# Dense products in column tiles behind a value block, in a two-layer attention and GLU kernel

## The chip, the cores and the metric

The kernel runs on one core of a Trainium2 chip. The metric is the device time of one execution in microseconds; a version's time is the median of three runs. A profile is taken of one further execution, and its trace gives the start of every instruction.

## What is computed

Two equal layers of sliding-window attention and a gated feed-forward part over 2,048 tokens of width 512, in bfloat16, with a layer norm without weights ahead of each part:

```python
def _A_ref(x, wqkv, wo):
    H = 32; Dh = D // H; W = 256          # D = 512, Dh = 16, S = 2048
    q, k, v = ...                          # x @ wqkv, by heads
    scores = jnp.einsum("bhqd,bhkd->bhqk", q, k) * (Dh ** -0.5)
    mask = (idx[:, None] - idx[None, :] >= 0) & (idx[:, None] - idx[None, :] < W)
    p = _softmax(jnp.where(mask[None, None], scores, -1e9), axis=-1)
    o = jnp.einsum("bhqk,bhkd->bhqd", p, v)
    return heads_joined(o) @ wo

def _B_ref(x, w_gate, w_up, w_down):       # F = 1792
    h = _sigmoid(x @ w_gate) * (x @ w_up)
    return h @ w_down

x = x + _A_ref(_layernorm(x), A_wqkv, A_wo)
x = x + _B_ref(_layernorm(x), B_w_gate, B_w_up, B_w_down)
x = x + _A_ref(_layernorm(x), A_wqkv, A_wo)
x = x + _B_ref(_layernorm(x), B_w_gate, B_w_up, B_w_down)
```

Both layers use the same weights. All weights and the residual `xsb` stay in SBUF for the whole run.

## The kernel before

**Tiles.** Tokens go in 16 tiles of 128 per layer. A query tile sees its own key tile and the two before it. PE (TensorE) works in three tilings:

- *dense products* use the whole 128 x 128 array: q and k (`q_unit` L768, `k_unit` L799), v (`v_unit` L838), gate and up (`glu_units` L863, product at L871), down (`down_units` L924, product at L935) and the output projection (`oproj_unit` L962, product at L966). One step is one matmul of 128, 256 or 512 columns; a unit's steps accumulate in one of four PSUM banks.
- *scores* (`scores` L1075) use four row tiles of 32 x 128, one for each of four heads' key slices, and write the tile `Sps`, four PSUM banks that all visits share. A *visit* is one such block for a key tile and a quarter of the heads (kind "A") or for the window's edges (kind "R"); there are 154 in the two layers. After each comes one exponential on ACT (L1155) over 128 x 2048 elements, which empties `Sps` into the ring `PTring` or into `edge`.
- *values* (`values` L1157, product at L1182) use four column tiles of 128 x 32: one block is 16 heads of one query tile, 80 matmuls (fewer for a layer's first two tiles) of 64 or 128 columns in groups of four, each with a `tile_position` of (0, 32g) and its own weights of 32 columns. There are 64 blocks.

Results leave the banks by copies on ACT or DVE, tanh on ACT and a fused multiply on DVE (L889, L897) for gate and up, and adds on DVE. Transposes of normed rows and of the attention's output go by DMA on SP's queue, but for the first tiles, which go by PE.

**Order.** No engine's order is written out by hand. While the program is built, a planner (`Plan`, L211) keeps a time for each engine with a table of costs, and each engine takes the ready task of the lowest priority number (`dispatch` L249). PE asks `pick` (L1279): a score visit if its inputs are there, the exponential before has ended and a pace has passed; else a value block whose probabilities are masked (`do_values` L1346), as a rule straight after a score visit; else one step of a dense unit from `choose` (L1414). The planner counts instructions, since PE's code comes in blocks of 256 (`count`, `held`, `issue`, L350 to L371), and it charges a fixed cost where the mode goes from one of "d", "s" and "pv" to another (`matmul` L391). The priorities, slacks, ranks and the pace are numbers in `SEGMENTS` (L94), with one set for the start of each stretch of visits; `OPT`, `RANK`, `EARLY` and `GLU` hold further choices. In the program that results, all that is fixed; at run time engines wait only for each other's semaphores.

The planner's numbers are what it plans with; they are not measurements.

The step of a dense unit, before:

```python
ns, fn = u.steps[u.at]
pl.count(1)
end = pl.matmul("d", ns)
fn()
```

Of the kernel before, what the change touches and what calls it, by code (L numbers as in the profile page):

```python
# [56 lines left out]
def pool_ns(n):  # L57
# [2 lines left out]

EXP_NS = 1880
TAIL = (384, 128)
GLU = [[[1, 1, 1, 1, 2, 2], [1, 1, 1, 1, 2, 2], [1, 1, 1, 1, 2, 2], [1, 1, 1, 1, 1, 1, 1, 1], [2, 2, 2, 2], [1, 1, 2, 2, 2], [2, 2, 4]], [[4, 4, 4, 2, 1, 1], [4, 4, 4, 1, 1, 2], [4, 4, 4, 4]]]
EARLY = 12
FILL = 800
OVERLAP = {"ACT": 114, "DVE": 83, "POOL": 45, "SP": 0}
LATENCY = {"ACT": 45, "DVE": 40, "POOL": 60, "SP": 0}
# [11 lines left out]
FETCH = (1200, 2300)  # L79


OPT = dict(gu='SP', g1=1, bk=3, bq=2, wide=0, r0=2, g0=2, g2=2, x0=1, eps=1, hold=0, own=1, ck=0, cq=2, turn=2,
    split=0, mo=0, r1=0, near=0)
RANK = dict(x3=33548.83335140428, wd=1211.7000995894928)


class Late(dict):


    def __missing__(self, name):  # L90
# [1 line left out]


SEGMENTS = {  # L94
    0: (False, dict(st_x0=13.863, ap_x0=3.152, xt_x0=9.296, st_x1=3.154, ap_x1=7.542, xt_x1=6.357, st_x=14.008,
        ap_x=13.772, xt_x=-3.395, st_p=0.711, ap_p=14.553, xt_p=4.622, st_g=-2.573, ap_g=-1.639, xt_g=-3.705,
        st_g0=2.021, ap_g0=-16.439, xt_g0=-6.334, tp=9.915, tp_g=2.607, q=-4.446, q0=12.608, q1=-11.166, k=-12.623,
        k0=2.155, k1=0.919, s=-5.392, s0=-1.662, s1=-1.49, v=5.412, v0=19.01, v1=20.238, vv=6.697, exp=-6.258,
        exp0=-3.822, m0=0.08, m00=3.447, e0=-5.468, e00=2.019, e1=3.572, e10=7.186, m2=1.966, m20=4.281, th=10.065,
        mu=-9.464, dn=-12.991, add=-5.529, add0=6.323, out=-9.784, mv=27.065, mv0=4.046, oq=-1.002, oq0=-4.981,  # L100
        no=2.541, no0=-9.565, on=10.323, on0=-6.623, vc=8.609, vc0=1.087), dict(xt=2480, oq=333, on=656, vc=2033),
        dict(tp=-12.366, o=-7.523, lead=12.467, far=66.411, v=2.907, g=58.132, d=22.245, feed=32.11,
        x3=33548.83335140428, wd=1211.7000995894928, go=147.06927590305332), 622.2),
    5: (False, {}, {}, {}, 622.2),
    10: (False, {}, {}, {}, 622.2),
    12: (False, {}, {}, {}, 2218.12),
    15: (False, {}, {}, {}, 2218.12),
    20: (False, {}, {}, {}, 2218.12),
    25: (True, dict(st_p=1.759, ap_p=37.537, xt_p=1.918, st_x=-0.666, ap_x=-8.548, xt_x=10.765, st_g=-9.429,
        ap_g=-8.046, xt_g=17.53, q=-9.886, k=11.998, s=-2.346, v=-6.167, exp=-28.375, m0=5.963, e0=7.951, e1=8.163,  # L110
        m2=6.893, th=-3.899, mu=-14.418, dn=5.971, add=-16.001, out=22.687, mv=28.405, oq=-3.007, no=5.357, on=9.644,
        vc=-13.067), dict(xt=205, oq=2779, on=3180, vc=6577), dict(tp=25.318, o=-33.126, lead=9.136, far=25.67, v=1.764,
        g=13.215, d=13.271, feed=-39.311, go=2154.735913081243), 2702.16),
    30: (False, {}, {}, {}, 2702.16),
    35: (False, {}, {}, {}, 2702.16),
    40: (False, {}, {}, {}, 2702.16),
    45: (False, {}, {}, {}, 2702.16),
    50: (False, {}, {}, {}, 2702.16),
    55: (False, {}, {}, {}, 2702.16),
    60: (False, {}, {}, {}, 2702.16),  # L120
    65: (False, {}, {}, {}, 2702.16),
    70: (False, {}, {}, {}, 2702.16),
    75: (False, {}, {}, {}, 2702.16),
    80: (False, {}, {}, {}, 2591.1),
    85: (False, {}, {}, {}, 3017.42),
    90: (False, dict(oq=-4.09), {}, dict(o=-30.75, lead=9.62, v=1.47), 2875.9),
    95: (False, dict(oq=-3.007), {}, dict(o=-33.126, lead=9.136, v=1.764), 3017.42),
    100: (False, {}, {}, {}, 3017.42),
    105: (False, {}, {}, {}, 3017.42),
    110: (False, {}, {}, {}, 3017.42),  # L130
    115: (False, dict(xt_x=13.72, m0=9.31), {}, {}, 2984.3),
    120: (False, dict(xt_x=10.765, m0=5.963), {}, {}, 3017.42),
    125: (False, {}, {}, {}, 3017.42),
    130: (False, {}, {}, {}, 3017.42),
    135: (False, {}, {}, {}, 3017.42),
    140: (False, {}, {}, {}, 3017.42),
    145: (False, {}, {}, {}, 3017.42),
    150: (False, {}, {}, {}, 3017.42),
}


# [270 lines left out]
class Net:  # L412


    def __init__(self, ctx, tc, A_x, wqkv, wo, w_gate, w_up, w_down, out):
# [37 lines left out]
        self.rms = [big.tile([P, 1], F32, name=f"rm{e}") for e in range(2)]  # L453
        self.bufs = {}
        self.slot = 0

        def ring(name, n, shape, dt=BF16):
            self.bufs[name] = [[big.tile(shape, dt, name=f"{name}{i}"), True] for i in range(n)]
# [306 lines left out]
    def cut(self, L, g, cq, n):  # L765
        return ((0, NBG - 1), (NBG - 1, 1)) if L == g == 0 and cq < n else ((0, NBG),)

    def q_unit(self, L, g, cq, i0, n):  # L768
        nc, pl, key = self.nc, self.pl, ("p", L, g)
        t0, gi = g * NBG + i0, L * NTG + g  # L770

        by_tile = L == g == 0 and cq < OPT["bq"]
        w = P if by_tile else n * P

        def steps(bank):
            return [(mm_ns(w), lambda kt=kt, o=o: nc.tensor.matmul(  # L776
                self.banks[bank][:, o:o + w], lhsT=self.wq[:, kt, cq * P:cq * P + P],
                rhs=self.xnT[key][0][:, i0 + o // P:i0 + (o + w) // P, kt, :],
                start=kt == 0, stop=kt == KT - 1)) for o in range(0, n * P, w) for kt in range(KT)]

        def evac(u):
            u.done.then(lambda: self.used(key, 1))
            at = gi % QG * TGW + i0 * P
            d = pl.task({"ACT": act_ns(n * P), "DVE": dve_ns(n * P)}, lambda e: self.copy(
                e, self.qT[:, cq, at:at + n * P].rearrange("p (t z k) -> p t z k", z=2, k=HP),
                self.banks[u.bank][:, 0:n * P].rearrange("p (t k z) -> p t z k", z=2, k=HP)), [u.done], self.prio["q" + self.phase(L, g)])
            d.done.then(lambda: [self.q_ready[L, t, cq].fire() for t in range(t0, t0 + n)])
            return d.done

        tiles = [self.xn_ready[key, t] for t in range(t0, t0 + n)]  # L790
        needs = [self.has_wq["q"]] + ([] if by_tile else tiles)
        if gi >= QG:
            needs.append(self.seen[divmod((gi - QG) * NBG + NBG - 1, NT)])
        u = Unit(("q", L, g, cq if i0 == 0 else cq + 3), steps, needs, False, evac)
        if by_tile:
            u.want = [e for e in tiles for kt in range(KT)]
        return u

    def k_unit(self, L, g, cq, i0, n):  # L799
# [4 lines left out]
        w = P if by_tile else n * P  # L804

        def steps(bank):
            return [(mm_ns(w), lambda kt=kt, o=o: nc.tensor.matmul(  # L807
                self.banks[bank][:, o:o + w], lhsT=self.wq[:, kt, D + cq * P:D + cq * P + P],
                rhs=self.xnT[key][0][:, i0 + o // P:i0 + (o + w) // P, kt, :],
                start=kt == 0, stop=kt == KT - 1)) for o in range(0, n * P, w) for kt in range(KT)]  # L810
# [27 lines left out]
    def v_unit(self, L, t):  # L838
# [1 line left out]
        key, gi, o = ("p", L, g), L * NTG + g, (t % NBG) * P  # L840

        def steps(bank):
            return [(mm_ns(D), lambda kt=kt: nc.tensor.matmul(  # L843
                self.banks[bank][:], lhsT=self.xnT[key][0][:, t % NBG, kt, :], rhs=self.wq[:, kt, 2 * D:3 * D],
                start=kt == 0, stop=kt == KT - 1)) for kt in range(KT)]

# [16 lines left out]
    def glu_units(self, L, t0, n, c0):  # L863
# [4 lines left out]

        def mms(bank, wts, fcs):
            pt = self.banks[bank][:, 0:len(wts) * len(fcs) * w].rearrange("p (i f w) -> p i f w", i=len(wts), w=w)  # L870
            return [(mm_ns(w), lambda i=i, j=j, fc=fc, wt=wt, kt=kt: self.nc.tensor.matmul(  # L871
                pt[:, i, j, :], lhsT=wt[:, kt, fc * P:(fc + 1) * P], rhs=self.xnT[key][0][:, q0:q0 + n, kt, :],
                start=kt == 0, stop=kt == KT - 1))
                for i, wt in enumerate(wts) for j, fc in enumerate(fcs) for kt in range(KT)]
# [49 lines left out]
    def down_units(self, L, t, t0, n, c0):  # L924
# [4 lines left out]
        def unit(o, w):  # L929
# [2 lines left out]

            def mm(bank, fc):
                at = (c0 * GW + fc * n * P + (t - t0) * P) % (HCH * GW)
                nc.tensor.matmul(self.banks[bank][:, 0:w], lhsT=self.hT[:, at:at + P], rhs=self.wd[:, fc, d],  # L935
                                 start=fc == 0, stop=fc == FC - 1)
                if t == t0 + n - 1 and end:
                    pl.at(pl.pe_free + PE_LATENCY, self.h_used[L, t0, fc].fire)
# [23 lines left out]
    def oproj_unit(self, L, t, b):  # L962
        nc, pl = self.nc, self.pl

        def steps(bank):
            return [(mm_ns(D), lambda c=c: nc.tensor.matmul(  # L966
                self.banks[bank][:], lhsT=b[0][:, c, :], rhs=self.wot[:, c, :],
                start=c == 0, stop=c == KT - 1)) for c in range(KT)]

# [309 lines left out]
    def pick(self):  # L1279
# [20 lines left out]
                    t < 2 or self.v_hi[L, t - 2].fired):  # L1300
                pv = self.pv_list[0]
        held = s < len(self.visits) and s > 0 and self.exps[s - 1].ends is None
        if visit and pl.mode == "pv" and go <= 0:
            if go > 0:
                return False
            wait = go
        elif pv and (pl.mode != "d" and 1 or wait <= -1 or wait > 1e8 or held):
            return self.do_values(pv, spare)
# [2 lines left out]
            u = self.choose()  # L1311
        if visit and (wait <= 0 or go <= 0 and u is None):
            self.last_s = pl.now
            end = pl.matmul("s", self.scores(*visit))
            pl.at(end, self.s_done[s].fire)
            self.exps[s] = self.visit_exp(s)
# [15 lines left out]
                return True  # L1332
            return False
        ns, fn = u.steps[u.at]
        pl.count(1)
        end = pl.matmul("d", ns)
        fn()
        u.at += 1
        if u.at == 1 and u.begin:
# [3 lines left out]
            pl.at(end, u.done.fire)  # L1343
        return True

    def do_values(self, pv, spare):  # L1346
        pl = self.pl
        self.pv_list.pop(0)
        bank = min(spare, key=lambda i: self.bank_turn[i])
        self.bank_user[bank] = Unit(("v alues",), None, [], False, None)  # L1350
        end = pl.matmul("pv", self.values(*pv, bank))
# [241 lines left out]
```

## Time and profile before

| | us |
|---|---|
| median of three runs | 540.58 |
| lowest, highest | 539.96, 541.48 |
| profiled execution: whole time | 542.07 |
| profiled execution: span of the trace | 540.4 |

The mean granted clock of TensorE in the profiled execution is 0.999. The profile's page cuts the span into 40 slices of 13.5 us; a digit is the busy share in tenths:

```profile
PE   6999999999999999999999999999999999999997
PEld 5446654866757544444444445444444445444443
DVE  5899989889897888678978978878967866552332
ACT  2999979978989798787787886788858774330320
```

PE is short of full in the first slice and the last alone. ACT and DVE are nearly full in the first third and have room afterwards; past some 455 us no visit is left, and PE runs dense products to the end. Engine names on the page: PE is TensorE's matmul, PEld its weight loads, DVE VectorE, ACT ScalarE, POOL GpSimd, SP the engine that issues most DMAs. The busy time of PE holds overlapping matmuls, so what a matmul costs is read from the distance of two starts.

The costliest groups on PE, by shape:

```profile
L935 PE MATMUL bank<-wd,hT 128*128 128x512 bf16 x434 | 105.7, 380 | 0.0
L871 PE MATMUL bank<-xnT,wu 128*128 128x512 bf16 x336 | 89.0, 379 | 0.0
L871 PE MATMUL bank<-xnT,wg 128*128 128x512 bf16 x336 | 87.8, 380 | 0.0
L1182 PE MATMUL bank<-PTring,Vaug 128*32 128x64 bf16 x1920 | 47.7, 193 | 0.0
L1182 PE MATMUL bank<-PTring,Vaug 128*32 128x128 bf16 x960 | 45.0, 223 | 0.0
```

The columns are line, engine, operation, tile written and tiles read, the array tile, the output's shape, the count, busy us and mean ns of one, and idle time before. The mean of 380 ns for a product of 512 columns includes the time from entry to end of one matmul; the next one starts long before that.

### The profile page before, as it was taken

To read this page: it belongs to the slowest core of one execution; us is meant where nothing else is said; L and a number is where in the kernel's file an instruction comes from. 1 tells how busy PE (TensorE), PEld (TensorE's weight loads), DVE (VectorE), ACT (ScalarE), POOL (GpSimd) and SP (SyncE) were. 2 spreads that over 40 slices of the span, in tenths; PEclk is the share of its full clock that TensorE was granted. 3 is DMA by queue.
4 is the path that set the end of the run, shared out by engine and by line. 5 is a ranking of instruction groups with operands and counts; after the bars stand their busy time and mean duration, and the time that the engine had idled before them with its cause. 6 is when DMAs were issued, how large, how long until landed. Compare 5 with 4: busy or idle time off the path is not lost.

```text
span 540.4 us, 21116 instructions
## 1 busy us (share of the span) xinstructions
PE 529.0 (98%) x9536; PEld 279.7 (52%) x9536; DVE 411.0 (76%) x820; ACT 385.9 (71%) x377; POOL 43.6 (8%) x99
## 2 busy tenths in 40 slices
PE   6999999999999999999999999999999999999997
PEld 5446654866757544444444445444444445444443
DVE  5899989889897888678978978878967866552332
ACT  2999979978989798787787886788858774330320
POOL 3411001000001010000000101001000001000000
PEclk9999999999999999999999999999999999999999
DMA  8843533224332225223112612062222512411001
GB/s 261 310 113 74 100 73 51 54 51 92 33 61 43 61 42 111 33 60 72 42 32 52 101 41 43 18 105 59 45 51 52 83 29 52 69 19 40 1 12 39
DMA packets 95083, 36.22 MB, mean 67 GB/s; under 512 B 78352, under 2 KB 93968, under 8 KB 94992
## 3 DMA queue, kind: packets, MB, share of 16 engines
q1 hardware_dynamic: 93872, 33.82, 29.7%
q8 instruction: 74, 1.21, 0.9%
q10 hardware_dynamic: 1120, 1.05, 0.7%
q14 instruction: 17, 0.14, 0.1%
HBM read 9.70 MB, written 2.10 MB: 22 GB/s over the span
## 4 chain that ended last, share of the span: by engine, by line
PE 90%; DMA 3%; ACT 3%; DVE 2%; issue 1%; SPq 1%; POOL 0%; ACTq 0%
PE bank L871 37%; PE bank L935 18%; PE bank L1182 8%; PE Sps L1102 7%; PE bank L966 5%; PE bank L776 4%; PE bank L807 4%; PE bank L843 4%; PE Sps L1113 2%; DMA xnT<-xn 2%; ACT PTring L1155 1%; DMA wq<-in_A_wqkv_dram 1%; SPq L527 1%; DVE st L645 0%; DVE PTring L1033 0%
## 5 line engine op out<-in xcount | busy, mean ns | idle before, releaser
L1155 ACT ACTIVATE PTring<-Sps 128x2048 bf16<-128x2048 f32 (+1 forms) x122 | 226.1, 1853 | 48.5 <-PE Sps L1102 44.0
L871 PE MATMUL bank<-xnT,wu 128*128 128x512 bf16 (+2 forms) x672 | 125.0, 308 | 0.0
L871 PE MATMUL bank<-xnT,wg 128*128 128x512 bf16 (+2 forms) x672 | 123.6, 309 | 0.4 <-DMA xnT<-xn 0.4
L897 DVE SCALAR_TENSOR_TENSOR hT<-hT,bank 128x512 bf16<-128x512 bf16 (+1 forms) x140 | 78.9, 576 | 44.7 <-PE bank L871 36.4
L889 ACT ACTIVATE hT<-bank 128x512 bf16<-128x512 f32 (+1 forms) x140 | 69.8, 514 | 56.3 <-PE bank L871 55.8
L935 PE MATMUL bank<-wd,hT 128*128 128x512 bf16 (+2 forms) x462 | 108.8, 373 | 0.0
L871 PEld LDWEIGHTS <-wu 128*128 128x128 bf16 x672 | 55.9, 98 | 40.5 <-issue 2.5
L871 PEld LDWEIGHTS <-wg 128*128 128x128 bf16 x672 | 55.0, 98 | 41.8 <-issue 3.0
L1155 ACT ACTIVATE edge<-Sps 128x2048 bf16<-128x2048 f32 (+1 forms) x32 | 56.8, 1774 | 16.5 <-PE Sps L1113 16.5
L935 PEld LDWEIGHTS <-hT 128*128 128x128 bf16 x462 | 42.6, 98 | 48.2 <-issue 1.2
L1033 DVE TENSOR_TENSOR PTring<-PTring,mask 128x1024 bf16<-128x1024 bf16 x64 | 43.6, 683 | 11.7 <-ACT PTring L1155 11.6
L1182 PE MATMUL bank<-PTring,Vaug 128*32 128x64 bf16 (+1 forms) x2880 | 51.5, 203 | 0.0
L1182 PEld LDWEIGHTS <-Vaug 128*32 128x32 bf16 x2880 | 43.8, 97 | 11.6 <-issue 9.5
L1102 PE MATMUL Sps<-qT,kTp 32*128 32x256 bf16 (+3 forms) x1216 | 47.4, 248 | 0.8 <-ACT edge L1155 0.4
L736 DVE CAST OTs<-bank 128x512 bf16<-128x512 f32 x50 | 36.4, 729 | 13.8 <-PE bank L1182 13.4
L645 DVE BATCH_NORM_STATS2 st<-xsb 128x6 f32<-128x512 bf16 x64 | 43.9, 687 | 3.4 <-DMA xsb<-in_A_x_dram 2.7
L658 POOL TENSOR_SCALAR st<-st 128x2 f32<-128x2 f32 (+1 forms) x33 | 11.3, 344 | 424.6 <-DVE st L647 424.4
L1182 PE MATMUL bank<-edge,Vl 128*32 128x64 bf16 x1024 | 44.4, 193 | 0.0
L1033 DVE TENSOR_TENSOR edge<-edge,maske 128x1024 bf16<-128x1024 bf16 x60 | 39.9, 681 | 1.3 <-ACT edge L1155 1.2
L1102 PEld LDWEIGHTS <-kTp 32*128 32x128 bf16 x1216 | 17.8, 92 | 44.0 <-issue 42.1
L1182 PE MATMUL bank<-edge,Vh 128*32 128x64 bf16 x896 | 40.6, 193 | 0.0
L1033 DVE TENSOR_TENSOR PTring<-PTring,maskn 128x1024 bf16<-128x1024 bf16 x56 | 38.2, 682 | 0.7 <-ACT PTring L1155 0.7
(76 smaller groups left out, 523.7 us busy)
## 6 DMA issues: line engine op xcount, KB each, us to landing
Vl<-Vaug SPq DMA_DIRECT2D x32, 68.0 KB, 2.7
out_dram<-xsb SPq DMA_DIRECT2D x15, 128.0 KB, 2.1
Vh<-Vaug SPq DMA_DIRECT2D x28, 68.0 KB, 2.6
wg<-in_B_w_gate_dram SPq DMA_DIRECT2D x2, 896.0 KB, 8.6
wu<-in_B_w_up_dram SPq DMA_DIRECT2D x2, 896.0 KB, 12.1
wd<-in_B_w_down_dram SPq DMA_DIRECT2D x7, 256.0 KB, 4.4
xsb<-in_A_x_dram SPq DMA_DIRECT2D x6, 256.0 KB, 7.0
wq<-in_A_wqkv_dram ACTq DMA_DIRECT2D x3, 256.0 KB, 5.7
```

The costliest lines, as they stand in the source:

```text
L645: nc.vector.bn_stats(out=st[:, 0:6], in_=self.xsb[:, t, :])
L736: self.nc.vector.tensor_copy(out=out, in_=in_)
L776: return [(mm_ns(w), lambda kt=kt, o=o: nc.tensor.matmul(self.banks[bank][:, o:o + w], lhsT=self.wq[:, kt, cq * P:cq * P + P], rhs=self.xn ...
L871: return [(mm_ns(w), lambda i=i, j=j, fc=fc, wt=wt, kt=kt: self.nc.tensor.matmul(pt[:, i, j, :], lhsT=wt[:, kt, fc * P:(fc + 1) * P], rhs= ...
L889: self.nc.scalar.activation(out=self.hT[:, ch[0] * GW:ch[0] * GW + size], in_=pt, func=AF.Tanh, scale=0.5)
L897: self.nc.vector.scalar_tensor_tensor(out=h, in0=h, scalar=1.0, in1=pt, op0=ALU.add, op1=ALU.mult)
L935: nc.tensor.matmul(self.banks[bank][:, 0:w], lhsT=self.hT[:, at:at + P], rhs=self.wd[:, fc, d], start=fc == 0, stop=fc == FC - 1)
L966: return [(mm_ns(D), lambda c=c: nc.tensor.matmul(self.banks[bank][:], lhsT=b[0][:, c, :], rhs=self.wot[:, c, :], start=c == 0, stop=c == ...
L1033: done = pl.task({"DVE": dve_bf_ns(1024)}, lambda e: nc.vector.tensor_tensor(out=r, in0=r, in1=m.to_broadcast([P, 16, HP]), op=ALU.mult), ...
L1102: nc.tensor.matmul(self.sps[:, m, o:o + n * HP], lhsT=kTp[32 * m:32 * m + 32, i, tt, e, :], rhs=self.qT[32 * m:32 * m + 32, i, q0:q0 + n * ...
L1155: nc.scalar.activation(out=out, in_=src, func=AF.Exp, scale=scale)
L1182: nc.tensor.matmul(o, lhsT=Va[:, c0:c0 + 32], rhs=p(h), start=k == 0 or t == 0, stop=k == len(parts) - 1 or t == 0, tile_position=(0, 32 * g))
```

## The change

Two things change. First, a dense step that is picked while PE is in the values' tiling (mode "pv"), with the next score visit less than `ranks["col"]` (about 2.5 us of the plan) away, is issued as four matmuls of 32 weight columns each, in the same four column tiles that values use, and PE's mode stays "pv". At most 16 such steps follow each other. Transposes on PE never run so. The products and their accumulation in the bank are the same. Second, the planner's numbers are others, so that all engines' orders are planned anew.

```diff
-GLU = [[..., [1, 1, 1, 1, 2, 2], [1, 1, 1, 1, 1, 1, 1, 1], ...]]
-EARLY = 12
+GLU = [[..., [1, 1, 1, 1, 1, 1, 2], [1, 1, 1, 1, 1, 1, 1, 1], ...]]
+EARLY = 8
...
-OPT = dict(gu='SP', g1=1, bk=3, bq=2, wide=0, r0=2, g0=2, g2=2, x0=1, eps=1, hold=0, own=1, ck=0, cq=2, turn=2,
-    split=0, mo=0, r1=0, near=0)
-RANK = dict(x3=33548.83335140428, wd=1211.7000995894928)
+OPT = dict(gu='SP', g1=1, bk=3, bq=2, wide=0, r0=2, g0=0, g2=2, x0=1, eps=1, hold=1, own=1, ck=0, cq=2, turn=2,
+    split=0, mo=0, col=16, near=0, r1=1)
+RANK = dict(x3=32849.91338862893, wd=1289.5079568774777)
...
+    def mm(self, out, lhsT, rhs, start, stop):
+        if not self.col:
+            self.nc.tensor.matmul(out, lhsT=lhsT, rhs=rhs, start=start, stop=stop)
+            return
+        for g in range(4):
+            q = slice(32 * g, 32 * g + 32)
+            self.nc.tensor.matmul(out[q], lhsT=lhsT[:, q], rhs=rhs, start=start, stop=stop, tile_position=(0, 32 * g))
...
-            return [(mm_ns(D), lambda kt=kt: nc.tensor.matmul(
+            return [(mm_ns(D), lambda kt=kt: self.mm(
...
-        if visit and pl.mode == "pv" and go <= 0:
-            if go > 0:
-                return False
+        if visit and pl.mode == "pv" and go <= 0 and not self.runs:
             wait = go
...
         ns, fn = u.steps[u.at]
-        pl.count(1)
-        end = pl.matmul("d", ns)
+        near = min(wait, go if self.pv_due() else 1e9)
+        self.col = pl.mode == "pv" and u.name[0] != "tp" and near < self.ranks["col"] and self.runs < OPT["col"]
+        self.runs = self.runs + 1 if self.col else 0
+        pl.count(4 if self.col else 1)
+        end = pl.matmul("pv" if self.col else "d", ns + 3 * self.col)
         fn()
...
+    def pv_due(self):
+        return False
```

The same exchange of `nc.tensor.matmul` for `self.mm` stands in the q, k, v, gate and up, down and output products. `runs` is set to 0 at a score visit and at a value block. `SEGMENTS` has new numbers throughout (for one, the pace at the first visits goes from 622 to 2463 and later from 3017 to 2914). The entry of `GLU` that `g0` names is the same list in both, so the token groups of gate, up and down are unchanged. `hold=1` lets the norm statistics of tiles 2 and 3 wait for tiles 0 and 1. `x3` and `wd` are when the last tokens and the pieces of the down weights are asked for: the last tokens at 32.8 us of the plan instead of 33.5, the last piece at 63.8 instead of 62.6.

## The prediction

> **What bounds the kernel now.** First the page: busy times, the queue that carries PE's code, the shares of the chain of waits, and the row of the exponentials.
>
> ```profile
> PE 529.0 (98%) x9536; PEld 279.7 (52%) x9536; DVE 411.0 (76%) x820; ACT 385.9 (71%) x377; POOL 43.6 (8%) x99
> ...
> q8 instruction: 74, 1.21, 0.9%
> ...
> PE 90%; DMA 3%; ACT 3%; DVE 2%; issue 1%; SPq 1%; POOL 0%; ACTq 0%
> ...
> L1155 ACT ACTIVATE PTring<-Sps 128x2048 bf16<-128x2048 f32 (+1 forms) x122 | 226.1, 1853 | 48.5 <-PE Sps L1102 44.0
> ```
>
> PE is busy 98% of the span and holds 90% of the chain; no other engine passes 76%. So the time is PE's own sequence plus what interrupts it, and every number below is a change of one of these two. The second line counts 74 loads of code. PE runs 2 x 9,536 = 19,072 loads and matmuls, 258 per code load.
>
> Next the timeline of PE over one round, since the change is about how PE goes from one tiling to another.
>
> ```profile
> 301.71 0.81 PE L871 MATMUL bank<-xnT,wu 128*128 128x512 bf16 x3
> 302.45 0.40 PE L1102 MATMUL Sps<-qT,kTp 32*128 32x256 bf16 x8
> 302.78 0.27 PE L1182 MATMUL bank<-PTring,Vaug 128*32 128x128 bf16 x8
> 302.87 0.20 PE L1182 MATMUL bank<-edge,Vh 128*32 128x64 bf16 x4
> 302.90 0.20 PE L1182 MATMUL bank<-PTring,Vaug 128*32 128x64 bf16 x4
> 302.93 0.20 PE L1182 MATMUL bank<-edge,Vl 128*32 128x64 bf16 x4
> 302.96 0.26 PE L1182 MATMUL bank<-PTring,Vaug 128*32 128x128 bf16 x8
> ...
> 303.45 0.20 PE L1182 MATMUL bank<-edge,Vl 128*32 128x64 bf16 x4
> 303.59 1.04 PE L871 MATMUL bank<-xnT,wg 128*128 128x512 bf16 x4
> 304.46 1.03 PE L871 MATMUL bank<-xnT,wu 128*128 128x512 bf16 x4
> 305.42 0.41 PE L1113 MATMUL Sps<-qT,kTp 32*128 32x64 bf16 x32
> ```
>
> The first column is the start, and starts are what counts, since matmuls overlap. Four dense 512-column products take 304.46 - 303.59 = 0.87 us, 0.216 each (the median over 1,391 such gaps). Four value products of 64 columns, one in each tile of 32 columns, take 0.029 (302.87 to 302.90). Where the tiling changes, the gap is longer: 303.45 to 303.59 is 0.14 where 0.03 would do. Over the trace, the starts on either side of a change put it above plain streaming by 111 ns for values to dense, 98 for dense to scores, 104 for scores to dense, 100 for scores to values, 110 for values to scores (one case).
>
> Third, an interruption on the same timeline:
>
> ```profile
> 59.64 0.61 PE L871 MATMUL bank<-xnT,wg 128*128 128x128 bf16 x8
> 60.09 0.61 PE L871 MATMUL bank<-xnT,wu 128*128 128x128 bf16 x8
> 60.53 0.27 PE L871 MATMUL bank<-xnT,wg 128*128 128x128 bf16 x2
> 60.74 0.26 PE L1113 MATMUL Sps<-qT,kTp 32*128 32x64 bf16 x10
> 61.73 0.35 PE L1113 MATMUL Sps<-qT,kTp 32*128 32x64 bf16 x22 [0.73 <-issue]
> ```
>
> At 60.8 PE stops 0.9 us in the middle of a score visit, waiting for nothing that the profile shows ("issue"). A load on the code queue began at 59.36 and ended at 60.28; PE went on 1.4 us later. The closest starts of two code loads in the trace are 3.48, 3.56 and 3.65 us apart. So 258 instructions can't go faster than about 3.6 us, and values followed by short products try to. The page's last line above sets a second floor: all visits write one score tile, so a visit waits for the exponential (1.85 us) of the one before; the shortest distance of two visits' starts in the trace is 2.41 us.
>
> I also laid the order of before out by these prices: streaming plus changes of tiling come to 522.3 us. Of what the trace has beyond that, 7.8 us lie before 28 us (start, first loads). After 28 us some 1.5 us are stops on code, 1.7 us are other waits (ACT, xnT, OnT) and 1.9 us are small change.
>
> **The change, part by part.** The program's order of after against before:
>
> 1. *Changes of tiling.* Before has 372, after 323. Values to dense fall from 58 to 6 (52 x 111 = -5.77 us), dense to scores from 151 to 99 (52 x 98 = -5.10), values to scores rise from 3 to 55 (52 x 110 = +5.72), scores to dense by 3 and scores to values fall by 3 (+0.01), dense to values rise by 3 (3 x 100 = +0.30). The sum is -4.84; the 49 plain gaps that come back at 2.5 ns make it **-4.7 us**. The price of values to scores rests on one case, but it lies beside values to dense (111).
>
> 2. *Dense products in column tiles.* 504 steps (362 of 512 columns, 67 of 256, 75 of 128) become four matmuls each; columns streamed stay equal. A dense step of 128 columns takes 56 ns (60.09 - 59.64 over 8). In the values' tiling, four matmuls of 128 columns and four of 64 take 85 to 90 ns (302.96 to the next row, left out, at 303.05), 29 of them for the 64, so again 56 to 58. I take 0. A column-tiled stream wider than 128 is not in the trace. Bounds: 504 x -2.5 = -1.3 us, if the step lost its gap; +5.5 us, if it behaved like the wide score groups (four of 256 columns in row tiles take 120 ns, 11 more than a dense 256): 504 x 11. I take 0 because columns are the nearer row.
>
> The Trainium skill speaks against this step: "TensorEngine Tiling (Array Packing)", section Instruction Overhead, says each matmul carries about 60 cycles and that the tiling factor should not come from a small dimension. At 2.4 GHz four would need 100 ns, so by it the 75 short steps would lose 44 ns each, 3.3 us (an estimate from that page). The trace's 29 ns for four matmuls contradict it, and the sum does without it.
>
> 3. *Code.* 1,512 more matmuls and as many weight loads are 3,024 instructions, 11.7 more code loads. PE's price per 258 instructions falls from 7.1 to 6.1 us on average, which hides them; what counts is where they crowd. Values (160 instructions in 0.70 us) are now followed by steps of eight instructions. I cut PE's order into pieces of the code loads' size and priced each by the rows above, with visits held 2.41 us apart. Before has four pieces under 5 us, the shortest 3.56. After has nineteen: 2.07, 2.40, 2.86, 2.97, 3.26, 3.54, 3.86, 3.90, and eleven from 4.07 to 4.92. At 3.6 us per load the first six lack 1.53 + 1.20 + 0.74 + 0.63 + 0.34 + 0.06 = 4.5 us, against before's 1.5 in the trace: **+3.0 us**. Bounds: -1.5 (all hidden) and +7.6, if each load needs 4.2 us (it took 4.7 from where PE came near the boundary to the end of the stop at 60.8): then the pieces lack 9.1. A stop on code holds everything behind it on PE, the next score visit first; that visit's exponential is then late too, which ACT (71% busy) can bear.
>
> 4. *The new order.* Its start is the same to 28 us, step for step. ACT, DVE, POOL and SP keep their work: 384 instructions on ACT for 385, 823 on DVE for 822, 104 on POOL and 190 on SP in both, transfers among them; who copies what and when is dealt anew. All of it is hidden under PE (71 and 76%) unless PE waits. After 28 us, ten distances between visits are now priced under 2.41 us: 2.18, 1.75, 2.26, 2.04, 2.27, 2.27, 1.54, 2.11, 2.05, 2.16. They lack 3.5 us in all, 1.3 of it at three places where code is late as well, so 2.2 remain. I add 0.7, less than half of the old other waits, for waits inside longer distances, and take off the old 1.7: **+1.2 us**. Bounds: 0 (they merely replace the old ones) and +2.2 (they come on top). The down weights' last piece is asked for at 63.8 us instead of 62.6 and lands some 4.4 us after; its product came at 69 us and comes about 71 now. Without that cover it costs 1.2 us at most.
>
> Sum: -4.7 + 0 + 3.0 + 1.2 = **-0.5 us**. The profiled execution took 542.07 us, 540.4 of it span; the median of three runs is 540.58, so the profile reads 1.5 us high and only the difference carries over: 540.58 - 0.5 = 540.1 us. Of this kernel a measurement can tell about 0.3% (1.6 us) from no change: faster means below 538.9, slower above 542.2.
>
> **The rivals.**
>
> *The saving stands* (faster). Code comes in time, because stops fall where PE waits for an exponential anyway, and the new waits half replace the old, so a third of step 3's 3.0 us and half of step 4's 1.2 are paid: -4.7 + 1.0 + 0.6 = -3.1, **537.5 us**. For it: three of the ten short distances already coincide, and a piece priced 3.56 us in before's trace passes without a stop. Against it: pieces of 2.1 and 2.4 us can't be met at any spacing that the trace shows. Chance 0.35.
>
> *Code loading decides* (slower). One mechanism: after a value block PE runs through its code faster than it is delivered. In before a load started up to 2 us after PE came near its boundary, most often just behind value blocks, where after puts its new instructions. At 4.1 us per load the pieces lack 8.0 us: -4.7 + 6.5 + 1.2 = +3.0, **543.6 us**. It decides from about 3.93 us per load on (a lack of 6.6). For it: 60.8 us in the trace. Against it: most loads there started 1.1 us after the boundary came near. Chance 0.21.
>
> *Column tiles stream slower when wide* (slower): the score groups' 11 ns per step, -0.5 + 5.5 = +5.0, **545.6 us**. Against it: their overhead stays at 2 to 3 ns from 64 to 128 columns. Chance 0.05.
>
> That the change does nothing is out: the order shows 2,016 dense matmuls in tiles of 32.
>
> **How the numbers follow.** The forecast, within 0.3%, has 0.37; other mishaps on the slow side 0.02. So faster 0.35, same 0.37, slower 0.28. The likeliest case's own range, 538.9 to 542.2, is the band. The range for 8 in 10 reaches halfway into both rivals' own spread, from 536.3 (-4.3: saving whole, 0.4 lost) to 543.6 (the code rival's time): about 0.1 stays out on either side.
>
> **What would show it.** Right: PE's gap behind a value block is one group's, not 0.14; a four-tile step of 512 columns takes 216 ns; some 86 code loads; PE waits after 28 us of about 7 us instead of 3, half of them "issue" between 90 and 120 us. Wrong: four-tile steps above 220 ns (step 2), waits under 4 us (the faster rival), code waits over 7 us (the slower), or dense products that wait on xnT or hT, which the sum doesn't hold.

## The result, and the profile after

The changed kernel is slower. Seven runs of each on the same chip gave medians of 546.07 us (544.58 to 547.16) for after and 541.48 us (539.96 to 543.49) for before: ratio 1.008, 95% interval 1.0055 to 1.0105. That is less than 2%, but clear of the scatter of the runs. The ratios, here and below, are estimated from all the runs and can differ from the quotient of the medians (1.0085 here); each experiment was measured beside before on one chip, not always the chip of the other experiments, so kernels are compared by their ratios to before. The profiled execution of after has a span of 544.3 us, before's had 540.4.

The page of after, with the lines that answer to those shown of before (busy time of each engine, the code queue, the shares of the chain of waits, the row of the exponentials):

```profile
PE 521.6 (96%) x10993; PEld 283.4 (52%) x11048; DVE 411.6 (76%) x821; ACT 385.4 (71%) x376; POOL 43.1 (8%) x99
...
q8 instruction: 86, 1.41, 1.1%
...
PE 84%; DVE 7%; ACT 3%; issue 3%; POOL 1%; DMA 1%; ACTq 0%; DVEq 0%
...
L1167 ACT ACTIVATE PTring<-Sps 128x2048 bf16<-128x2048 f32 (+1 forms) x122 | 225.9, 1852 | 46.9 <-PE Sps L1114 42.3
```

PE's share of the chain fell from 90 to 84%, "issue" rose from 1 to 3% and DVE from 2 to 7%. Code loads rose from 74 to 86. The other engines' work is nearly unchanged. (55 of the 11,048 matmuls have no record; they were placed by their weight loads.) The timeline of PE over one round, at the place that the change is about:

```profile
297.34 0.20 PE L1194 MATMUL bank<-PTring,Vaug 128*32 128x64 bf16 x4
297.37 0.20 PE L1194 MATMUL bank<-edge,Vl 128*32 128x64 bf16 x4
297.39 0.39 PE L778 MATMUL bank<-xnT,wu 128*32 128x512 bf16 x4
297.61 1.04 PE L778 MATMUL bank<-xnT,wg 128*32 128x512 bf16 x16
298.48 0.61 PE L778 MATMUL bank<-wd,hT 128*32 128x512 bf16 x8
298.91 0.39 PE L778 MATMUL bank<-xnT,wu 128*32 128x512 bf16 x4
299.23 0.40 PE L1114 MATMUL Sps<-qT,kTp 32*128 32x256 bf16 x8
```

The step behind the value block starts 0.02 to 0.03 us after it (297.37 to 297.39), not 0.14. Sixteen matmuls of 512 columns are four steps and take 298.48 - 297.61 = 0.87 us, the same as four whole products before. The change of tiling has moved to the scores: 298.91 to 299.23 is 0.32 us, 0.216 of it streaming. So the edit does what it says, at the price foreseen. What went wrong is in the waits of PE. Before has one row of "issue" in that view, of 0.7 us, and none of its waits for exponentials is longer than 0.4:

```profile
PE Sps L1113 <- issue: 0.7, 1, 0.7
PE Sps L1102 <- ACT edge L1155: 0.4, 1, 0.4
```

After, the longest sums:

```profile
PE bank L774 <- issue: 5.3, 21, 1.4
PE bank L778 <- issue: 1.4, 2, 0.8
PE bank L1194 <- issue: 1.2, 2, 1.0
...
PE Sps L1125 <- issue: 0.8, 1, 0.8
PE bank L1194 <- DVE PTring L1045: 0.8, 1, 0.8
```

Each row is what waited, for what, us in total, times, longest. The first row has seeming waits of 0.16 us too, behind products whose record is missing. One of the "issue" rows' waits on the timeline:

```profile
107.91 0.62 PE L778 MATMUL bank<-xnT,wu 128*32 128x128 bf16 x32
108.46 0.34 PE L774 MATMUL bank<-xnT,wg 128*128 128x128 bf16 x3
108.73 0.40 PE L1114 MATMUL Sps<-qT,kTp 32*128 32x256 bf16 x8
110.54 0.44 PE L774 MATMUL bank<-xnT,wg 128*128 128x128 bf16 x5 [1.41 <-issue]
```

Behind eight short tiled steps (32 matmuls in 0.55 us), three short whole ones and a score visit PE stands for 1.4 us and waits for nothing shown. A load on the code queue ended at 109.29, 1.26 us before PE went on.

I laid PE's order out by the prediction's prices and sorted what each trace has beyond them: the time to 28 us; stops on code; waits of over 0.15 us that the profile names, after 28 us; the rest. About 4.9 us at both ends of the span are the same in all. By this sort before has 1.1 us of code stops and 1.2 us of named waits, where the prediction counted 1.5 and 1.7. The table has the kernels of the experiments too:

| us | span | priced work | to 28 us | code stops | named waits | rest |
|---|---|---|---|---|---|---|
| before | 540.4 | 522.3 | 7.8 | 1.1 | 1.2 | 3.1 |
| after | 544.3 | 517.6 | 6.8 | 8.3 | 3.8 | 2.9 |
| E1: new order, no tiles | 548.4 | 522.6 | 6.8 | 3.6 | 6.1 | 4.5 |
| E2: old order, all tiles | 552.6 | 517.4 | 8.0 | 15.8 | 3.9 | 2.8 |
| E7: new order, chosen tiles | 541.0 | 519.8 | 7.6 | 0.0 | 5.9 | 2.8 |
| E8: old order, chosen tiles | 538.9 | 519.0 | 8.3 | 0.6 | 3.4 | 2.7 |

Before to after: -4.7 of priced work, +7.2 of code stops, +2.6 of named waits, -1.0 at the start and -0.2 of rest make +3.9 us, the difference of the spans.

### The profile page after: what moved, and what is told of

It is laid out like the page before. It is cut to its first block, busy times and chain, and to the rows that moved or that the text cites. A ratio compares the mean times of both kernels' runs of the same rounds, so it can differ in the third digit from the quotient of the medians.

```text
span 544.3 us, 24074 instructions
## 1 busy us (share of the span) xinstructions
PE 521.6 (96%) x10993; PEld 283.4 (52%) x11048; DVE 411.6 (76%) x821; ACT 385.4 (71%) x376; POOL 43.1 (8%) x99
## 3 DMA queue, kind: packets, MB, share of 16 engines
q10 hardware_dynamic: 1120, 1.05, 0.6%
## 4 chain that ended last, share of the span: by engine, by line
PE 84%; DVE 7%; ACT 3%; issue 3%; POOL 1%; DMA 1%; ACTq 0%; DVEq 0%
PE bank L774 52%; PE bank L778 15%; PE bank L1194 8%; PE Sps L1114 6%; ACT PTring L1167 2%; PE Sps L1125 2%; DVE st L649 1%; DVE PTring L1045 1%; DMA xsb<-in_A_x_dram 1%; DVE kTp L834 1%; POOL st L663 1%; DVE xn L681 1%; DVE edge L1045 1%; DVE xsb L984 0%; DVE kTp L740 0%
## 5 line engine op out<-in xcount | busy, mean ns | idle before, releaser
L774 PE MATMUL bank<-xnT,wu 128*128 128x512 bf16 (+2 forms) x552 | 102.0, 307 | 0.3 <-issue 0.2
L774 PE MATMUL bank<-xnT,wg 128*128 128x512 bf16 (+2 forms) x518 | 96.2, 309 | 2.4 <-issue 2.2
L774 PE MATMUL bank<-wd,hT 128*128 128x512 bf16 (+2 forms) x349 | 81.5, 371 | 2.4 <-issue 1.3
L1167 ACT ACTIVATE edge<-Sps 128x2048 bf16<-128x2048 f32 (+1 forms) x32 | 56.7, 1771 | 13.3 <-PE Sps L1125 12.7
L774 PEld LDWEIGHTS <-wu 128*128 128x128 bf16 x552 | 45.8, 98 | 34.9 <-issue 2.8
L774 PEld LDWEIGHTS <-wg 128*128 128x128 bf16 x518 | 42.9, 98 | 36.2 <-issue 5.4
L774 PEld LDWEIGHTS <-hT 128*128 128x128 bf16 x376 | 35.3, 98 | 40.3 <-issue 2.1
L774 PE MATMUL bank<-xnT,wq 128*128 128x512 bf16 (+1 forms) x256 | 48.7, 330 | 0.6 <-DMA wq<-in_A_wqkv_dram 0.4
```

The costliest lines, as they stand in the source:

```text
L774: self.nc.tensor.matmul(out, lhsT=lhsT, rhs=rhs, start=start, stop=stop)
L1167: nc.scalar.activation(out=out, in_=src, func=AF.Exp, scale=scale)
```

## The experiments

E1 to E4 ask which part of the change costs the time, E5 to E10 test a rule for the stops that came out of the first traces.

**E1: the new order without column tiles.** After, with the branch for four tiles switched off; the order of all engines is after's.

```diff
-        if not self.col:
+        if True:
             self.nc.tensor.matmul(out, lhsT=lhsT, rhs=rhs, start=start, stop=stop)
             return
```

Expected: 

> The new order kept instruction for instruction, but every dense product issued on the whole array again: 1,512 matmuls and 1,512 weight loads fewer, 375 changes of tiling instead of 323. Theory (code arrives late): the changed kernel's stops at the code boundaries, 8.3 us in its trace, fall to 1.5 or less, the tiling costs 5.0 us more by the trace's prices (522.6 instead of 517.6 us), so 1 to 2 us less than the changed kernel: about 544 us, some 2 us over before, which is what the new order's other waits cost. Rival (the new order's own waits make the loss, not the tiles): the loss of 8.6 us in waits stays and 5.0 us come on top, about 551 us.

Measured: 550.16 us against 542.64, ratio 1.0138 (1.0118 to 1.0159). So the first theory's 544 us is out and the rival's 551 is met: the new order without the tiles that it was planned with costs more than the whole change. The rival's number is met, but only part of its account: of the 8.0 us that E1's span has over before's, 4.9 are named waits, 2.5 are code stops and most of the rest is matmuls at a lower clock. Its priced work is before's, and it has 6.1 us of named waits instead of 1.2: a mask that a value block waits for at 44 us (0.80), transposes that wait for their sources between 45 and 48 us (1.3 in sum), an exponential at 111 us (0.89), a dense step at 95.5 us (1.2). One code stop of 2.3 us is followed by a stretch of matmuls at half speed. In the view of PE's waits:

```profile
PE bank L1194 <- issue: 2.4, 2, 2.1
PE Sps L1114 <- ACT PTring L1167: 1.8, 5, 0.8
```

**E2: column tiles in the old order.** Before, with every dense step between a value block and the next visit (at most 16 of them, no transposes) in four tiles. These are 542 steps, 2,168 tiled matmuls in the trace; where the expectations of E8 and E9 say 532, it is 542.

```diff
+        self.tiles = 0 if u.name[0] == "tp" else max(self.tiles - 1, 0)
         fn()
...
         self.pv_list.pop(0)
+        self.tiles = 17
```

Expected: 

> The order of before kept, and the dense steps behind a value block (at most 16, until a score visit or a transpose) issued in four column tiles: 1,626 matmuls more than before, 321 changes of tiling instead of 372, priced 517.4 instead of 522.3 us. Theory (code arrives late): the old order was not made for the extra code, so stops at the code boundaries grow by 8 to 17 us; less 4.9 us for the tiling, 545 to 553 us. Rival (the new order's waits make the loss): the saving of 4.9 us shows, about 536.5 us.

Measured: 554.12 us, ratio 1.0219 (1.02 to 1.0237). Priced work falls by 4.9 us as in after, and code stops rise to 15.8 us at fourteen places. The rival's gain is out; the tiles without the new order are worse still, and the reason is code.

**E3: after with code moved.** Each of the 54 warm-up products, which compute nothing, is cut in two: 108 more instructions ahead of everything, the rest of PE's order untouched.

```diff
-        for i in range(n):
-            nc.tensor.matmul(self.banks[bank][:, 0:P], lhsT=self.hT[:, 0:P], rhs=self.hT[:, 0:P], start=True, stop=True)
+        for i in range(2 * n):
+            nc.tensor.matmul(self.banks[bank][:, 0:P // 2], lhsT=self.hT[:, 0:P], rhs=self.hT[:, 0:P // 2], start=True, stop=True)
```

Expected: 

> The changed kernel with each of the 54 warming products of the start (128 columns) split into two of 64: 108 instructions more ahead of everything, the same work on the array, so the code blocks' boundaries fall 0.42 of a block elsewhere in an otherwise equal order. Theory (code arrives late): the stops leave their places (99, 103, 110, 118, 178, 222, 275 us) and reappear where the shifted boundaries lie, again 0.8 of a block in; their sum stays between 5 and 11 us, the time within 4 us of the changed kernel. Rival (the stops belong to the work at those places): same places, same lengths, same time within 0.3%.

Measured: 552.83 us, ratio 1.0201 (1.0168 to 1.0234), some 6.5 us above after, where at most 4 were expected. Code stops are 10.2 us instead of 8.3, all at other places (99.9: 1.75, 111.9: 1.56, 467.1: 1.91 us). Counted in PE's loads and matmuls, though, they lie where those of after lie: at the same remainder over 256. So what counts is where blocks of 256 instructions end. Code is only 1.9 us of the 7.0 that the span gains over after's. Another 2.0 us are there before the first value block (at 31.3 us instead of 29.3), ahead of any stop, and waits of visits for exponentials (the rows of `PTring` and `edge`) grow from 1.7 to 3.2 us.

**E4: two column tiles of 64.** After with half as many matmuls per tiled step.

```diff
-        for g in range(4):
-            q = slice(32 * g, 32 * g + 32)
-            self.nc.tensor.matmul(out[q], lhsT=lhsT[:, q], rhs=rhs, start=start, stop=stop, tile_position=(0, 32 * g))
+        for g in range(2):
+            q = slice(64 * g, 64 * g + 64)
+            self.nc.tensor.matmul(out[q], lhsT=lhsT[:, q], rhs=rhs, start=start, stop=stop, tile_position=(0, 64 * g))
```

Expected: 

> The changed kernel with the tiled dense steps as two column tiles of 64 instead of four of 32: two loads and two matmuls per step, 1,008 matmuls fewer. If going from tiles of 32 to tiles of 64 columns is no change of tiling, the saving of 4.7 us stays and the code stops fall from 8.3 to some 3 us: about 541 us. If it is one, there are 379 changes, 56 x 0.1 us come on top of the changed kernel and the code stops fall: about 546 us with stops of 3 us, and the starts on either side of values to dense lie 0.14 us apart as before.

Measured: 551.92 us, ratio 1.0174 (1.0138 to 1.0211). The timeline at the place shown of after:

```profile
301.76 0.20 PE L1194 MATMUL bank<-PTring,Vaug 128*32 128x64 bf16 x4
301.79 0.20 PE L1194 MATMUL bank<-edge,Vl 128*32 128x64 bf16 x4
301.93 0.41 PE L778 MATMUL bank<-xnT,wu 128*64 128x512 bf16 x2
302.17 1.03 PE L778 MATMUL bank<-xnT,wg 128*64 128x512 bf16 x8
```

The gap of 0.14 us is back: going from tiles of 32 to tiles of 64 columns is a change of tiling, 96 ns above streaming in the median of 56 places. That takes back the saving of step 1 (priced work 522.6 us). Code stops are 3.6 us; one of 2.4 us is followed by 3 us at a granted clock of 0.50. So the changes of tiling and the code came as in the second case of the expectation, but its 546 us are passed by 6. The expectation left out the slow clock; in the profile, a start that is 2.6 us longer (the first value block at 31.9 us instead of 29.3, with a wait of 2.7 us for `wq` instead of 0.4); and waits for exponentials of 2.9 us, as in E1 (in after 1.7).

**A rule for the stops.** In the traces of before, after and E1 to E3 I compared the starts and ends of the code loads with PE's position. Call the place where all stops lie the end of a block (the count of loads and matmuls gives 188 over 256 there early in the span, 182 late). When PE is about 30 instructions short of the end of one block, it asks for the block after the next (this is inferred from the starts of the loads); with PE running fast the load starts 1.05 us later (median; 0.64 to 1.47 in nine of ten cases without other transfers) and takes 1.1 us (0.9 to 1.4). PE can't pass the end of the next block before 1.4 us after that load's end (70 stops in the traces of all kernels but E4: 1.22 to 1.76, median 1.40). That makes 3.55 us for the 286 instructions from one asking to the end of the following block. This is a usual value, not a bound: stretches that ended in a stop took from 3.03 us (E3, stop at 134.6) to 5.7 us (E9, at 64.0), mostly as the load started early or late. Time won earlier is of no use, since in these traces PE never has more than the block that it runs and the next one: no load starts before its asking point. At 110.54 us above: PE came by the asking point at 106.86, the load started at 107.92 and ended at 109.29, PE was at the block's end at 109.06 and stood for 1.48 us.

Laid over PE's priced order, the rule gives a sum of stops for each kernel. For the first six it was worked out after their runs. For E5 to E10 the expectations, on record before the runs, have 2.3 us (E5, one stop), no stop where E5 has one (E6), under 1.5 (E7), 0.5 to 3.5 (E8), 8.4 (E9) and 13.8 (E10):

| | loads + matmuls | code stops by rule, us | in the trace, us |
|---|---|---|---|
| before | 19,072 | 0.1 | 1.1 |
| after | 22,096 | 5.3 | 8.3 |
| E1 | 19,072 | 2.5 | 3.6 |
| E2 | 22,324 | 16.5 | 15.8 |
| E3 | 22,204 | 9.3 | 10.2 |
| E4 | 20,080 | 2.5 | 3.6 |
| E5 | 19,120 | 2.4 | 3.2 |
| E6 | 19,264 | 0.1 | 0.4 |
| E7 | 20,584 | 0.0 | 0.0 |
| E8 | 21,130 | 0.2 | 0.6 |
| E9 | 22,452 | 8.4 | 12.7 |
| E10 | 21,258 | 13.8 | 14.1 |

**E5 and E6: one run of eight steps, and four.** The code of E2 with a table that says how many steps of each run behind a value block are tiled. E5 has 8 for run 50 alone, E6 for runs 50 to 53; all else is before.

```diff
+KEEP = [0] * 50 + [8] + [0] * 7
...
+        self.runs = self.runs + 1 if self.tiles else 0
+        self.run += self.runs == 1
-        if not self.tiles:
+        if not self.tiles or self.runs > KEEP[self.run]:
```

Expected of E5: 

> Before's order with a single run of eight 512-column steps (the one behind the value block at about 406 us) in four column tiles: 48 more instructions, nothing else. Theory (code comes one block of 256 instructions at a time: a load starts some 1.05 us after PE is 30 instructions short of a block's end, takes 1.1 us, and PE goes on 1.4 us after it, so the next 286 instructions can't pass in under 3.55 us, and slack before them doesn't help): nothing happens at the run itself (-0.1 us), but every later block's end moves by 48 instructions, and one of them then falls into a value block near 465 us, where no instruction differs from before: a stop of 2.3 us there, 60 us behind the edit. Time of before +2.2 us (bounds +1.5 to +3.5), ratio about 1.004. Rival (the four-tile steps cost the time where they stand): no stop at 465 us, 0.0 to +0.3 us.

Measured: 546.85 us against 541.68, ratio 1.0077 (1.0049 to 1.0104). The timeline of PE some 55 us behind the edit, where every instruction is before's. First before, then E5:

```profile
458.81 0.21 PE L1182 MATMUL bank<-edge,Vh 128*32 128x64 bf16 x4
458.84 0.21 PE L1182 MATMUL bank<-PTring,Vaug 128*32 128x64 bf16 x4
458.87 0.21 PE L1182 MATMUL bank<-edge,Vl 128*32 128x64 bf16 x4
459.02 0.82 PE L935 MATMUL bank<-wd,hT 128*128 128x512 bf16 x3
459.68 1.03 PE L871 MATMUL bank<-xnT,wg 128*128 128x512 bf16 x4
```

```profile
459.65 0.27 PE L1197 MATMUL bank<-PTring,Vaug 128*32 128x128 bf16 x8
459.74 0.21 PE L1197 MATMUL bank<-edge,Vh 128*32 128x64 bf16 x4
462.07 0.21 PE L1197 MATMUL bank<-PTring,Vaug 128*32 128x64 bf16 x4 [2.11 <-issue]
462.10 0.21 PE L1197 MATMUL bank<-edge,Vl 128*32 128x64 bf16 x4
462.61 1.06 PE L777 MATMUL bank<-wd,hT 128*128 128x512 bf16 x2 [0.30 <-issue]
463.47 1.91 PE L777 MATMUL bank<-xnT,wg 128*128 128x512 bf16 x4
```

The foretold stop is there, 2.30 us beyond the price, at 462 us instead of "near 465". Two value blocks of 160 instructions follow each other at this place, and 48 instructions more have moved a block's end into the second. The stop costs more than itself: the four products at 463.47 start 0.43 us apart, not 0.216. The windows of that stretch (us of PE busy, then of the other engines, the granted clock, share and rate of DMA):

```profile
455.00:460.00 5.00, 4.90 (x168) 2.78 (x167) 3.84 (x8) 2.05 (x2) 1.57 (x2) 1.00 0.18 46
460.00:465.00 5.00, 2.63 (x14) 1.12 (x15) 1.79 (x4) 0.90 (x2) 0.00 (x0) 0.73 0.49 82
465.00:470.00 5.00, 5.00 (x23) 2.15 (x22) 1.38 (x2) 1.66 (x3) 0.00 (x0) 0.93 0.35 79
```

The granted clock is down to 0.73 and then 0.93, which comes to some 3.4 us at half speed (1.7 us of clock lost; an estimate from these two rows). Seven products take 0.21 us longer each: 1.5 us on top of 2.3, which the expectation left out, so the median is 5.2 us over before's (4.2 by the ratio) instead of 1.5 to 3.5. Of the six executions one has a mean clock of 0.999 and took 543.31 us, 1.6 over before's median; the other five have 0.992 to 0.994 and took 546.19 to 547.25. So the stop alone costs about what was foretold, and the rest goes with the clock.

Expected of E6: 

> As the run before it, but with four runs of eight steps in column tiles (at about 406 to 431 us), 192 more instructions. Theory: the block's end near 465 us is moved on past the value block, so the stop of the run before it is gone although four times as many steps are tiled: -0.4 us against before (bounds -0.5 to +0.8), ratio about 0.999. Rival (tiled steps cost in proportion): four times what the run before it costs, so +8 us if that one costs 2.

Measured: 541.86 us, ratio 0.9998 (0.9978 to 1.0017), span 538.4. With four times the tiled steps the stop is gone. No fixed cost by the step or by the instruction can do that.

**E7 and E8: tile only where code has time.** In the order of after (E7) and of before (E8) the table `KEEP` was chosen, among many, by the rule's sum of stops: runs are tiled whole, not at all, or in their first steps only, so that this moves the ends of later blocks to a better place.

```diff
-        if not self.col:
+        if not self.col or self.runs > KEEP[self.run]:
```

Expected of E7: 

> After's order, unchanged, with 252 of the 504 steps in column tiles and 252 whole; which runs are tiled is chosen so that, by the rule of 286 instructions per 3.55 us, no block's end falls where code is late. Theory: changes of tiling cost 2.2 us more than in after (519.8 us of priced work instead of 517.6), the 8.3 us of code stops fall to under 1.5, and the other waits and the start stay: span 544.3 + 2.2 - 8.3 + 0.7 = 539 us (537.5 to 541), ratio to before 0.995 to 1.001. Rival (the new order's own waits and the steps' tiles cost the time; stops only move): 543 us or more, ratio over 1.005.

Measured: 543.15 us, ratio 1.002 (1.0003 to 1.0038), span 541.0. The code stops are gone to the last one. The time lies between the theory's ratio (up to 1.001) and the rival's (over 1.005), because the rest of the expectation fails: named waits are not 3.8 us, as in after, but 5.9. In the view of PE's waits (the "issue" row's 0.16 us each follow a product whose record is missing, so none is a stop):

```profile
PE bank L777 <- issue: 2.5, 16, 0.2
...
PE Sps L1117 <- ACT PTring L1170: 1.6, 4, 0.8
PE Sps L1117 <- ACT edge L1170: 1.1, 2, 0.6
...
PE bank L777 <- ACT Vaug L741: 0.7, 1, 0.7
PE bank L1197 <- DVE PTring L1048: 0.6, 1, 0.6
PE bank L1264 <- DVE OTs L743: 0.6, 1, 0.6
```

Most of these stand in E1 too. At 111.09 us a visit waits 0.88 us for the exponential; in after PE had stood 1.48 us on code just before that visit, and the exponential was done by then. So part of after's 8.3 us on code only covered waits that the new order has anyway: 2.1 us by the difference of the sums (5.9 - 3.8), of which this one place was followed.

Expected of E8: 

> Before's order, unchanged, with 343 of its 532 steps behind value blocks in column tiles, chosen by the same rule. Theory: priced work 519.0 instead of 522.3 us, code stops 0.5 to 3.5 us instead of 1.1: before's span of 540.4 becomes 536.5 to 539.5 us, ratio 0.993 to 0.998, faster than both kernels. Rival (stops grow with the number of tiled steps, 15.8 us for all 532): some 10 us of stops, 546 us or more, ratio over 1.01.

Measured: 539.85 us, ratio 0.9958 (0.9941 to 0.9975), span 538.9: faster than before and than after. It keeps 3.3 us of the 4.9 that E2 saved in priced work, at 0.6 us of code stops. 1.4 us of its 3.4 us of named waits are one dense step at 306.9 us that waits on a transfer; before has no such wait there, and its cause wasn't followed.

**E9 and E10: the same 128 instructions in two kernels.** Warm-up products in two pieces, the first ten in three, ahead of E2 (E9) and of E8 (E10).

```diff
+            self.warm += 1
+            for a, b in ((0, 48), (48, 88), (88, P)) if self.warm <= 10 else ((0, 64), (64, P)):
+                nc.tensor.matmul(self.banks[bank][:, a:b], lhsT=self.hT[:, 0:P], rhs=self.hT[:, a:b], start=True, stop=True)
```

Expected of E9: 

> The kernel with before's order and all 532 steps behind value blocks in column tiles (the one that took 554.1 us), with 128 more instructions ahead of everything: each of its 54 warm-up products, which compute nothing, is cut into two pieces, ten of them into three. Theory (286 instructions per 3.55 us, counted from where a block of 256 ends): the blocks' ends fall elsewhere, and the rule gives 8.4 us of code stops instead of 16.5: the kernel with more instructions is 8 us faster, 546 us (543 to 550), ratio about 1.007 instead of 1.022. Rival (stops go with the number of instructions, or with the tiled steps): 554 us or more.

Measured: 551.97 us, ratio 1.02 (1.0157 to 1.0243), against E2's 1.0219: no gain that the intervals can tell. Code stops fell, from 15.8 to 12.7 us, but not to 8.4: of thirteen loads that PE stood for, nine started 1.48 to 3.33 us after the asking point instead of 1.05, two of these after a stop that held PE itself. Waits on two transfers (1.3 us at 215, 1.2 at 374) took what was left. So the rule's sum is no forecast where many blocks are close to the limit: it came out 4.3 us too low here, 3.0 too low for after and 0.7 too high for E2.

Expected of E10: 

> The same 128 instructions ahead of the kernel with before's order and chosen runs in column tiles (the one that took 539.9 us). Theory: the choice was made for other block ends, and the rule gives 13.8 us of code stops instead of 0.2, two of them of 2.3 us, after which the clock may drop: 539.9 + 13.6 = 553 us (549 to 558), ratio 1.017 to 1.03. Rival (fewer tiled steps, fewer stops): 541 us, ratio 0.998.

Measured: 556.21 us, ratio 1.0277 (1.0246 to 1.0307), against E8's 0.9958. The same program, with 128 instructions of no use ahead, takes 3% longer; 14.1 us of code stops, 13.8 by the rule. One of them, inside a value block:

```profile
236.09 0.26 PE L1198 MATMUL bank<-PTring,Vaug 128*32 128x128 bf16 x6
237.88 0.21 PE L1198 MATMUL bank<-PTring,Vaug 128*32 128x64 bf16 x2 [1.53 <-issue]
237.89 0.23 PE L1198 MATMUL bank<-edge,Vh 128*32 128x64 bf16 x4
```

## Why the prediction was wrong

The forecast was 540.1 us; after is 1.008 times before, or 544.9 us on the scale of the runs shown. The cause is the one that the rival "code loading decides" named; its sum was 543.6.

1. *Changes of tiling, -4.7 us: right.* Priced work is 4.74 us less, every kind of gap is as priced, and E4, which brings a change back at 56 places, has 5.0 us of it again.
2. *Column tiles, 0 us: right.* Steps of 512, 256 and 128 columns take 216, 109 and 56 ns, as whole ones do. The Trainium skill's 60 cycles per matmul ("TensorEngine Tiling (Array Packing)", section Instruction Overhead) don't add up over the four tiles here: four matmuls of 128 columns take 56 ns, not 100. The 100 ns were the prediction's own estimate, which let the four follow each other; the page doesn't say that matmuls in different tiles do.
3. *Code, +3.0 us: the step that failed, by its size; it measured +7.2.* The prediction cut PE's order into pieces of the code loads' size and let each cost 3.6 us. Two things were wrong with that. First, what sets a stop is the time from an asking point to the end of the following block, 286 instructions, and where that end falls to within some tens of instructions: 48 make 2.3 us (E5), 128 make 13.5 (E8 to E10). By the rule the same prices give 5.3 us for after, where the pieces gave 4.5. Second, loads start late: of the ten longest stops in after (0.2 to 1.5 us), four had loads that started 0.98 to 1.14 us after the asking point, six had 1.4 to 2.8. With 1.05 us for these too, the ten would be some 4 us shorter. Two of the six follow another stop; for the other four (169.8, 179.4, 222.4 and 275.9 us) no cause is shown. In three of them, all but 222.4, no other transfer was moving between the asking point and the load's start. At 169.8 and 179.4 PE ran slow products there, so that the asking point itself, known to some tens of instructions, is uncertain. So of the 4.2 us that the step falls short, 0.8 is where the blocks end (5.3 - 4.5), 3.0 is what the trace has beyond the rule, which the late loads cover, and 0.4 is before's own stops (1.1, not 1.5).
4. *The new order's waits, +1.2 us: mis-sized too.* In after they are 2.6 us more than in before; with code out of the way 4.7 (E7), and 4.9 without any tiles (E1). The step looked at distances between visits alone. What it left out: a value block that waits for its mask at 44 us, transposes that wait for their sources up to 48 us, and, in E1 and E7, a dense step at 95.5 us. The start, taken as equal, was 1.0 us shorter; it is 7.1 and 9.1 us in E6 and E5, whose instructions there are the same, so this says nothing.

Two readings of the prediction are slightly off, without weight in its sum: the price per 258 instructions falls to 6.0 us, not 6.1 (517.6 us over 22,096 instructions), and the closest starts of two code loads in before are 3.48, 3.57, 3.60 and 3.65 us apart.

Of the signs named beforehand, the gap behind the value block, the 216 ns and the 86 loads came as written. PE's waits after 28 us are 12.1 us and not 7, 3.6 us of them on code between 90 and 120 us, and the code waits passed the 7 us that were to mean the slower rival. The saving-stands rival needed two thirds of step 3's stops to fall where PE waits anyway. The coincidence is real, but worth 2.1 of 8.3 us.

So both halves of the change are a loss by themselves (E1 +1.4%, E2 +2.2%), together they lose 0.8%, and the tiles alone, put where code has time, gain 0.4% (E8). The losses of the halves aren't fixed prices: E1's holds 3.6 us of code stops, which depend on where its blocks happen to end.

What stays open: what makes a code load start up to 2 us late, which is most of what step 3 lacked; why some transfers came later in E8 and E9 than in before.

The Trainium skill has the mechanism, in "Runtime: NRT & Kernel Launch", section Instruction fetch mechanics: code is fetched in blocks of 256 instructions, the next one while the current one runs. The traces agree. It adds that this is hidden, because instructions are dispatched more slowly than blocks are filled; 160 instructions of a value block in 0.70 us, and the 8.3 us of stops in after, say otherwise.

## What to carry to other kernels

An edit that multiplies instructions is paid where the time per block is shortest, not on average: lay the blocks' ends over the order and look at the few stretches in which a block and a bit take less than about 3.6 us. There an edit may cost nothing at its own place and microseconds far behind it, so a kernel near this limit has to be measured or planned again after every change of its instruction count, and an experiment on it has to tell an edit's own cost from that of the shift. A gain in streaming is worth taking first where PE's instructions are slow.

## What the hardware showed that I had not expected

Stops on code fall at one place in a block and end 1.40 us (1.22 to 1.76) after a load's end; in these traces nothing is fetched further ahead than one block, however long PE has been slow before. A stop of 2.3 to 2.4 us may be followed by a half clock (E4: 0.50 over 3 us; E1 and E5: windows that come to some 3.4 us at a half), or not (E10: 2.35 us, clock 1.00), and in E5 five of six executions show the lower clock and one doesn't. Tiles of 32 and of 64 columns count as different tilings (96 ns).
